# Moving the block-edge part of a short convolution from TensorE to Pool: raw edge tokens as a ninth block, seven taps summed in channel-major form

## The chip, the cores and the metric

One NeuronCore of one Trainium2 chip runs the whole program. The metric is the device time of one execution in microseconds (us), the median of several runs. The profile is taken from one execution; its span (first to last instruction) is some 1.7 us shorter than that execution's time. All runs quoted here are of the state called fast. Engines are named as in the profile: PE (TensorE), PEld (its weight loads), DVE (VectorE), ACT (ScalarE), POOL (GpSimd), SP (the queue that issues most transfers).

## The reference, cut to what matters

```python
# x: 8 x 4096 x 192, weight: 8 heads x 7 taps
w = softmax(weight, axis=-1)
x_pad = 6 zero tokens ahead of each sequence
out[b, s, head] = sum over k of w[head, k] * x_pad[b, s + k, head]   # causal, 7 taps
h = out.reshape(32768, 192) @ w_in       # 192 x 2048
return (h * cos(h)) @ w_out              # 2048 x 192
```

Each output token of the convolution needs the six tokens before it. That is what makes the edge of a block of 128 tokens special: the first six tokens of a block need tokens of the block before.

## The kernel before: the parts that the change touches

A tile is 512 tokens, a unit two tiles (8 blocks of 128 tokens). Per unit the steps are: load `x` and the 16 tokens around each block start; cast to bf16 (Pool); convolve with banded weights (PE); evict to `ct` (ACT copies the result out of PSUM, the memory that PE writes to); double (Pool); transpose by DMA to channel-major `cT`; repair the edges (Pool). Then `mm1` multiplies by `w_in`, ACT and DVE form h cos(h), and the second product runs on PE. Convolution, first product and second product of different tiles are interleaved by hand in `PE_ORDER`.

A convolution matmul sees one block at a time. The six tokens at each block start come out wrong, so the 8 starts of a unit, 16 tokens each, were convolved as a ninth block, and the right values copied over after the transpose:

```python
def mm(i, rows, **flags):
    return conv_mm(u, c, ps, i, sides[rows], 0, UB + 1, ...)        # 9 blocks, 216 columns
...
conv_out(u, c, ps, 0, 0, UB + 1, nc.scalar.copy, banks=(b,))         # ACT evicts 9 blocks

def double_unit(u, n0=0, n1=UB + 1):
    ct = ct_tiles[u]
    nc.gpsimd.tensor_copy(out=ct[:, n0:n1, :, 1, :], in_=ct[:, n0:n1, :, 0, :])

def mend_edges(u):                                                   # "the repair"
    nc.gpsimd.tensor_copy(out=cT[u][:, 0:UB, :, 0 : K - 1],
                          in_=cT[u][:, UB].rearrange("p c (n t) -> p n c t", t=16)[:, :, :, 8 : 8 + K - 1])

PE_ORDER = "h0 m1 c1 m6 c2 m4 h1 m10 h2 p h3 m10 h4 m9 h5 m9 h6 m4 q h7 m11"
```

## Time and profile before

| | before |
|---|---|
| time, median of 3 runs | 715.89 us (715.42 to 716.17) |
| span of the profiled run | 714.0 us |
| PE, DVE, ACT, POOL busy | 99%, 91%, 84%, 21% |
| PE clock granted | full throughout |
| steady tile | 10.83 us |

The prediction below shows the lines on which it rests. Two more views belong beside them. The first lists what PE's matmuls waited for in the whole run (us in total, times, longest us); its largest rows are:

```profile
PE h L349 <- DVE g L360: 1.4, 4, 0.5
PE o_ps L105 <- DVE zero L100: 1.3, 1, 1.3
PE o_ps L190 <- POOL x_bf L179: 0.8, 1, 0.8
```

All of these lie in the first 40 us. The second view is the table of stretches: length and busy time of each engine, then the granted clock (the column before the last two, 1.00 is full), DMA share and GB/s. It covers the moment at which tile 2 begins, in the kernel before:

```profile
34.00:38.00 4.00, 3.52 (x60) 2.56 (x58) 3.72 (x4) 3.80 (x6) 0.50 (x1) 1.00 0.90 113
38.00:43.00 5.00, 5.00 (x80) 3.62 (x78) 4.63 (x5) 4.11 (x5) 0.52 (x2) 1.00 0.89 197
```

### The profile page before, as it was taken

To read this page: it belongs to the slowest core of one execution; us is meant where nothing else is said; L and a number is where in the kernel's file an instruction comes from. 1 tells how busy PE (TensorE), PEld (TensorE's weight loads), DVE (VectorE), ACT (ScalarE), POOL (GpSimd) and SP (SyncE) were. 2 spreads that over 40 slices of the span, in tenths; PEclk is the share of its full clock that TensorE was granted. 3 is DMA by queue.
4 is the path that set the end of the run, shared out by engine and by line. 5 is a ranking of instruction groups with operands and counts; after the bars stand their busy time and mean duration, and the time that the engine had idled before them with its cause. 6 is when DMAs were issued, how large, how long until landed. Compare 5 with 4: busy or idle time off the path is not lost.

```text
span 714.0 us, 26320 instructions
## 1 busy us (share of the span) xinstructions
PE 704.0 (99%) x11826; PEld 539.5 (76%) x11827; DVE 647.6 (91%) x601; ACT 600.7 (84%) x718; POOL 149.4 (21%) x123
## 2 busy tenths in 40 slices
PE   7999999999999999999999999999999999999998
PEld 3577777777777777777777777777777777777776
DVE  7899999999999999999999999999999999999995
ACT  7888888888888888888888888888888888888874
POOL 5622111222102221202221122221022221121000
PEclk9999999999999999999999999999999999999999
DMA  8963554454763444553646543545644545513402
GB/s 215 233 146 85 134 146 107 113 123 97 146 134 103 129 101 119 145 123 100 141 88 133 145 108 111 129 91 145 137 90 138 103 117 146 127 50 90 95 25 68
DMA packets 183696, 85.24 MB, mean 119 GB/s; under 512 B 111648, under 2 KB 183200, under 8 KB 183584
## 3 DMA queue, kind: packets, MB, share of 16 engines
q1 hardware_dynamic: 182872, 82.59, 48.3%
q8 instruction: 92, 1.51, 0.9%
q0 software_dynamic: 416, 0.79, 0.8%
q10 hardware_dynamic: 296, 0.20, 0.1%
q14 instruction: 20, 0.16, 0.1%
HBM read 31.36 MB, written 25.17 MB: 79 GB/s over the span
## 4 chain that ended last, share of the span: by engine, by line
PE 96%; DVE 1%; ACT 1%; DMA 1%; POOL 1%; issue 0%; SPq 0%; POOLq 0%
PE o_ps L393 47%; PE h L349 45%; PE h L190 3%; DMA x_f<-in_x_dram 1%; ACT cs L356 0%; PE h L393 0%; POOL x_bf L179 0%; DVE g L360 0%; DVE band L279 0%; SPq L253 0%; POOL mask L128 0%; ACT mask L133 0%; ACT ct L298 0%; PE o_ps L190 0%; DVE diag L269 0%
## 5 line engine op out<-in xcount | busy, mean ns | idle before, releaser
L360 DVE TENSOR_TENSOR g<-h,cs 128x1024 bf16<-128x1024 f32 (+1 forms) x513 | 608.6, 1218 | 29.1 <-ACT cs L356 25.2
L356 ACT ACTIVATE cs<-h 128x1024 bf16<-128x1024 f32 (+1 forms) x513 | 514.0, 1022 | 99.8 <-PE h L349 93.7
L393 PE MATMUL o_ps<-wo,g 64*128 64x192 bf16 x8128 | 436.6, 243 | 1.2 <-ACT ct L205 0.6
L393 PEld LDWEIGHTS <-g 64*128 64x128 bf16 x8192 | 368.4, 94 | 86.6 <-SPq L164 1.1
L349 PE MATMUL h<-cT,w 64*128 64x512 bf16 (+1 forms) x3078 | 412.4, 376 | 1.9 <-DVE g L360 1.4
L349 PEld LDWEIGHTS <-w 64*128 64x128 bf16 x3078 | 161.1, 94 | 69.2 <-issue 3.4
L259 POOL COPY cT<-cT 128x144 bf16<-128x144 bf16 x31 | 9.5, 307 | 427.6 <-DMA cT<-ct 280.6
L179 POOL CAST x_bf<-x_f 128x1728 bf16<-128x1728 f32 (+1 forms) x32 | 80.4, 2514 | 8.0 <-DMA x_f<-in_x_dram 7.9
L247 POOL COPY ct<-ct 128x1728 bf16<-128x1728 bf16 x31 | 50.4, 1627 | 78.1 <-ACT ct L205 78.1
L404 DVE COPY o_sb<-o_ps 128x384 f32<-128x384 f32 x63 | 35.1, 558 | 26.1 <-PE o_ps L393 25.8
L205 ACT CAST ct<-h 128x432 bf16<-128x432 f32 x120 | 56.5, 522 | 0.6 <-PE h L190 0.3
L190 PE MATMUL h<-x_bf,band 64*128 64x216 bf16 (+1 forms) x472 | 43.4, 253 | 0.0
L404 ACT COPY o_sb<-o_ps 128x384 f32<-128x384 f32 x63 | 29.9, 474 | 1.6 <-PE o_ps L393 1.6
L190 PEld LDWEIGHTS <-band 64*128 64x128 bf16 (+1 forms) x496 | 24.3, 94 | 8.7 <-issue 1.5
L105 PE MATMUL o_ps<-zero 128*128 128x512 bf16 x12 | 4.3, 511 | 1.3 <-DVE zero L100 1.3
L105 PEld LDWEIGHTS <-zero 128*128 128x128 bf16 x15 | 1.5, 115 | 3.0 <-DVE zero L100 1.3
L414 DVE COPY o_sb<-h 128x192 f32<-128x192 f32 x1 | 0.4, 357 | 3.7 <-PE h L393 3.7
L414 ACT COPY o_sb<-h 128x192 f32<-128x192 f32 x1 | 0.3, 318 | 3.8 <-PE h L393 3.8
L461 POOL CAST wo<-wo_f 128x1536 bf16<-128x1536 f32 x2 | 2.9, 1470 | 1.8 <-DMA wo_f<-in_moe_w_out_dram 1.8
L393 PE MATMUL h<-wo,g 64*128 64x192 bf16 x64 | 3.0, 243 | 0.1
L190 PE MATMUL o_ps<-x_bf,band 128*128 128x96 bf16 (+1 forms) x24 | 1.9, 223 | 0.8 <-POOL x_bf L179 0.8
L292 PE MATMUL o_ps<-x_bf,band 128*128 128x48 bf16 x32 | 1.4, 183 | 1.2 <-ACT x_bf L179 0.7
(52 smaller groups left out, 32.3 us busy)
## 6 DMA issues: line engine op xcount, KB each, us to landing
out_dram<-o_sb SPq DMA_DIRECT2D x63, 384.0 KB
x_f<-in_x_dram SPq DMA_DIRECT2D x31, 768.0 KB
x_f<-in_x_dram SPq DMA_DIRECT2D x31, 96.0 KB
wo_f<-in_moe_w_out_dram SPq DMA_DIRECT2D x4, 384.0 KB
x_f<-in_x_dram SPq DMA_DIRECT2D x2, 384.0 KB
w<-in_moe_w_in_dram POOLq DMA_DIRECT2D x2, 384.0 KB, 6.3
cT<-ct SPq DMA_TRANSPOSE x32
out_dram<-o_sb ACTq DMA_DIRECT2D x2, 96.0 KB
```

The source lines that it names most:

```text
L105: nc.tensor.matmul(out=bank, lhsT=zero[:, 0:128], rhs=zero, start=True, stop=True)
L179: copy(out=bf[u][:, n0 + o : n1 + o, :].rearrange("p n (h k r) -> p (n h) k r", k=NC, r=R), in_=x_tiles[u][:, n0:n1, :].rearrange("p n (h ...
L190: return nc.tensor.matmul(out=ps[i // 2][:, 0 : (n1 - n0) * 2 * G].rearrange("p (n k i r) -> p i n k r", n=n1 - n0, k=NC, i=2)[:, i % 2], ...
L205: copy(o[:, :, 0, :], i[:, :, 0, :])
L247: nc.gpsimd.tensor_copy(out=ct[:, n0:n1, :, 1, :], in_=ct[:, n0:n1, :, 0, :])
L259: nc.gpsimd.tensor_copy(out=cT[u][:, 0:UB, :, 0 : K - 1], in_=cT[u][:, UB].rearrange("p c (n t) -> p n c t", t=16)[:, :, :, 8 : 8 + K - 1])
L349: nc.tensor.matmul(out=h[:, i, n0 * 128 : n1 * 128], lhsT=w[rows, k, j, :], rhs=c[rows, m0 + n0 : m0 + n1, k, :], start=(k == 0), stop=(k ...
L356: nc.scalar.activation(out=cs[:, :, part], in_=h[:, :, part], func=AF.Sin, bias=math.pi / 2.0, scale=1.0)
L360: nc.vector.tensor_tensor(out=g_tiles[t][:, 2 * j : 2 * j + 2, part], in0=h[:, :, part], in1=cs[:, :, part], op=ALU.mult)
L393: ms.append(nc.tensor.matmul(out=o_ps[tt, b, si], lhsT=g_tiles[tt][rows, f, s * 128 : (s + 1) * 128], rhs=wo[rows, f // 2, f % 2, :], star ...
L404: copies[b](o_sb[t][:, 2 * b : 2 * b + 2, :].rearrange("p s d -> p (s d)"), o_ps.pop((t, b)))
L461: nc.gpsimd.tensor_copy(out=wo[:, q * HP : (q + 1) * HP], in_=wo_f[:, q * HP : (q + 1) * HP])
```

## The change

The intent: take the ninth block out of PE's matmuls and ACT's evictions, since PE sets the time, and use Pool, which stood idle 79% of the span. The raw edge tokens are copied to `ct` and transposed with the rest; Pool then forms the seven-tap sums of the first six tokens of each block. The taps, by channel, come from two tiny matmuls at the start. The orders of the steady work were adjusted. The core of the diff, with cuts:

```diff
-            return conv_mm(u, c, ps, i, sides[rows], 0, UB + 1, ...)
+            return conv_mm(u, c, ps, i, sides[rows], 0, UB, ...)
-            conv_out(u, c, ps, 0, 0, UB + 1, nc.scalar.copy, banks=(b,))
+            conv_out(u, c, ps, 0, 0, UB, nc.scalar.copy, banks=(b,))
-        nc.gpsimd.tensor_copy(out=ct[:, n0:n1, :, 1, :], in_=ct[:, n0:n1, :, 0, :])
+        nc.gpsimd.tensor_copy(out=ct[:, 0:UB, :, 1, :], in_=ct[:, 0:UB, :, 0, :])
+        for t in range(2):
+            nc.gpsimd.tensor_copy(out=ct[:, UB, :, t, :]..., in_=bf[u][:, UB, :]...)
+    def spread_taps(ps):
+        for i in range(2):
+            nc.tensor.matmul(out=ps, lhsT=pick[:, i]..., rhs=wn[:, i, :], start=i == 0, stop=i == 1, ...)
+        nc.vector.tensor_copy(tap, ps)
     def mend_edges(u):
-        nc.gpsimd.tensor_copy(out=cT[u][:, 0:UB, :, 0 : K - 1], in_=cT[u][:, UB]...[:, :, :, 8 : 8 + K - 1])
+        window = ...                                  # 24 edges x 6 tokens x 7 taps, overlapping
+        nc.gpsimd.tensor_tensor(out=edge_prod, in0=window, in1=tap..., op=ALU.mult)
+        nc.gpsimd.tensor_tensor(out=edge_prod[..., 0:3], in0=edge_prod[..., 0:3], in1=edge_prod[..., 3:6], op=ALU.add)
+        for j in (1, 2):
+            nc.gpsimd.tensor_tensor(out=edge_prod[..., 0], in0=edge_prod[..., 0], in1=edge_prod[..., j], op=ALU.add)
+        nc.gpsimd.tensor_tensor(out=cT[u][:, 0:UB, :, 0 : K - 1]..., in0=edge_prod[..., 0], in1=edge_prod[..., 6], op=ALU.add)
@@ conv_rest (start-up)
+        spread_taps(banks[1][:, 2 * NB * 2 * G :][:, 0:K])
-    PE_ORDER = "h0 m1 c1 m6 c2 m4 h1 m10 h2 p h3 m10 h4 m9 h5 m9 h6 m4 q h7 m11"
-    ACT_ORDER = "s0 ec1 ec2 Q s1 P s2 s3 s4 s5 s6 s7"
+    PE_ORDER = "h0 m4 c1 m6 c2 m4 h1 m7 h2 p h3 m13 h4 m10 h5 m6 h6 m3 q h7 m11"
+    ACT_ORDER = "s0 ec1 Q ec2 s1 P s2 s3 s4 s5 s6 s7"
```

## The prediction

> **What bounds the kernel now.** I read the page first, for shares of the span. Its first and fourth parts:
>
> ```profile
> PE 704.0 (99%) x11826; PEld 539.5 (76%) x11827; DVE 647.6 (91%) x601; ACT 600.7 (84%) x718; POOL 149.4 (21%) x123
> PE 96%; DVE 1%; ACT 1%; DMA 1%; POOL 1%; issue 0%; SPq 0%; POOLq 0%
> ```
>
> TensorE is busy 99% of the span and carries 96% of the chain that ended last. Pool is the idle engine (21%). A busy TensorE isn't proof by itself, since matmul ends are modelled, so next I took the chain in order of time over one steady tile (a tile is 512 tokens, two tiles are one unit of 1024 tokens):
>
> ```profile
> 314.88 0.65 PE h L349 x6
> 315.52 0.08 PE o_ps L393 x2
> 315.61 0.18 PE h L190 x4
> 315.79 0.50 PE o_ps L393 x12
> 316.29 0.18 PE h L190 x4
> 316.47 0.33 PE o_ps L393 x8
> 316.80 0.65 PE h L349 x6
> ```
>
> Here the chain holds nothing but matmuls, back to back: L349 is the first matrix product, L393 the second, L190 the convolution. It also gives true spacings, which the mean durations don't, as two half-array matmuls run side by side. Twelve L393 matmuls of 192 columns take 0.50 us, so a pair takes 83 ns; six L349 of 512 columns take 0.65 us, a pair 217 ns; four L190 of 216 columns take 0.18 us, a pair 92 ns. A tile has 64 pairs of L393, 24 of L349 and 4 of L190: 5.28 + 5.19 + 0.37 = 10.84 us, and the tile before starts at 304.05, 10.83 us earlier. So in the steady part every pair counts and nothing else does. The costs there are spacings of pairs.
>
> Third, the groups by form, for durations on the engines the change touches (busy us and mean ns after the bar):
>
> ```profile
> L205 ACT CAST ct<-h 128x432 bf16<-128x432 f32 x120 | 56.5, 522 | 0.6 <-PE h L190 0.3 <-issue 0.3
> L247 POOL COPY ct<-ct 128x1728 bf16<-128x1728 bf16 x31 | 50.4, 1627 | 78.1 <-ACT ct L205 78.1
> L190 PE MATMUL h<-x_bf,band 64*128 64x216 bf16 x464 | 42.3, 253 | 0.0
> L259 POOL COPY cT<-cT 128x144 bf16<-128x144 bf16 x31 | 9.5, 307 | 427.6 <-DMA cT<-ct 280.6 <-PE h L349 147.0
> ```
>
> Last, Pool in order of time, in the steady part and then near the start, with TensorE beside it at the start. Columns: start us, duration us, what, and idle time before it.
>
> ```profile
> 300.42 0.31 POOL L259 COPY cT<-cT 128x144 bf16<-128x144 bf16 x1 [13.71 <-DMA cT<-ct]
> 300.67 2.57 POOL L179 CAST x_bf<-x_f 128x1728 bf16<-128x1728 f32 x1
> 306.68 1.63 POOL L247 COPY ct<-ct 128x1728 bf16<-128x1728 bf16 x1 [3.12 <-ACT ct L205]
> 322.06 0.31 POOL L259 COPY cT<-cT 128x144 bf16<-128x144 bf16 x1 [13.75 <-DMA cT<-ct]
> ```
>
> ```profile
> 20.52 1.47 POOL L461 CAST wo<-wo_f 128x1536 bf16<-128x1536 f32 x1 [1.78 <-DMA wo_f<-in_moe_w_out_dram]
> 21.93 1.63 POOL L247 COPY ct<-ct 128x1728 bf16<-128x1728 bf16 x1
> 28.20 2.54 POOL L179 CAST x_bf<-x_f 128x1728 bf16<-128x1728 f32 x1 [0.21 <-DMA x_f<-in_x_dram]
> 32.40 0.31 POOL L259 COPY cT<-cT 128x144 bf16<-128x144 bf16 x1 [1.66 <-DMA cT<-ct]
> ```
>
> ```profile
> 32.67 0.82 PE L393 MATMUL o_ps<-wo,g 64*128 64x192 bf16 x16
> 33.33 0.81 PE L349 MATMUL h<-cT,w 64*128 64x512 bf16 x6
> 36.52 0.82 PE L349 MATMUL h<-cT,w 64*128 64x512 bf16 x6 [0.48 <-DVE g L360]
> ```
>
> The steady repair of edges (L259) at 322.06 serves a unit whose first product starts near 336.5 (304.05 + 3 x 10.83): 14 us of slack. The very first repair does not have that. It serves unit 1, waits for that unit's transpose until 32.40, and the first product of tile 2, which reads unit 1, starts at 33.33, only 0.6 us after the repair's end at 32.71. There an instruction on the idle engine is almost on the path.
>
> **What the Trainium skill says.** "TensorE: Matmul & The Clock Gate", section "Back-to-back issue gap", gives an isolated warm gap of N/2.4 + 2.5 ns for N columns: 82.5, 215.8 and 92.5 ns for 192, 512 and 216. The trace's pairs (83, 217, 92) agree. "GPSIMD Engine Reference", section "3.1 Elementwise — side-by-side cycle accounting", gives 4497 ns for a two-input operation of 2048 fp32 elements per partition; no such operation is in this trace. The same page's section 7 adds some 50% per element for reads at a byte step over 8. "SBUF — State Buffer", section "Who interferes with whom", says that VectorE with at most one SBUF input outside the 2-port modes doesn't contend with Pool. VectorE's product L360 reads one operand from PSUM, and the trace agrees: four of them took 4.74 us from 298.35, while Pool cast during the second half, and 4.74 us again from 307.93, most of it with Pool idle.
>
> **The change, part by part.** (1) Convolution matmuls cover 8 blocks and not 9, 192 columns and not 216. A pair gets 10 ns cheaper (24 columns at 2.4 per ns; L393 has this very shape, at 83 ns). 464 half-array matmuls are 232 pairs: 232 x 10 ns = 2.3 us off the path. The 16 full-array ones of the first two tiles lie in a part where TensorE waits anyway: nothing.
>
> (2) ScalarE's evictions shrink from 432 to 384 elements. Its eviction of 384 from PSUM (L404) takes 474 ns against 522: 48 ns x 120 = 5.8 us, on an engine that is 84% busy and off the path: nothing.
>
> (3) The doubling on Pool copies 8 blocks (1536 elements) and adds two copies of 192. From 1728 elements in 1627 ns and 144 in 307 ns: 0.833 ns per element and 187 ns fixed. So 1467 + 2 x 347 = 2161 ns, 0.5 us more than 1.63.
>
> (4) The repair becomes a product of 24 x 6 x 7 = 1008 elements, an addition of 432 and three of 144. An estimate from the GPSIMD page and the fixed 187 ns of this trace: (4497 - 187) / 2048 = 2.10 ns per element. Product 187 + 2117 = 2.30 us; first addition 1.09; the three small ones read every seventh fp32, a step of 28 bytes, so half as much again per element: 187 + 144 x 3.15 = 0.64 each, 1.92 together. Sum 5.3 us; successive Pool instructions overlap by about 0.06 us in this trace, four times: 5.1. Without the stride penalty it is 4.6. I take 4.9 us, against 0.31.
>
> (5) Pool's sum per unit of 21.7 us: 4.9 + 2.55 + 2.16 = 9.6 us against 4.5. That is 44%, and in the steady part the longer repair ends near 327 instead of 322.4, the cast at 329.5, the doubling at 331.7; the transpose that needs it isn't issued before 337.62. No steady wait.
>
> (6) At the start, Pool's work in order: the doubling of unit 1 starts at 21.93 (set by the arrival of wo_f, unchanged) and ends 0.5 us later. The transpose is issued and lands 0.5 us later: 32.9. The repair runs to 37.8. The first product of tile 2 can't start before 37.85 instead of 33.33: 4.5 us. Everything before it on TensorE has room now, so slips there cost nothing more. Is any of it regained? The wait of 0.48 us at 36.52 is for the ring of three h buffers: first product, cosine (ScalarE), multiplication (VectorE), 3.19 us after that product's start. It moves along, so no. After it TensorE has no waits in which to make up time: +4.5 us on the end.
>
> (7) Later start-up: the doubling of unit 2 runs 37.8 to 40.0, its transpose 40.0 to 44.7 (4.72 as now), its repair about 48 to 53; needed at 54.77 + 4.5 = 59.3. The turn of the second product's row halves goes through the same queue as the transpose; it is needed near 47, so it is free. The taps' picking matrix (one memset, two selects, about 1.0 us by the rows of ident and mask) fits Pool's idle 1.66 us before 14.81. The two tiny matmuls and the 0.17 us copy of the taps fall before 33 us, behind the new wait.
>
> (8) The reordering. By the spacings above the ring needs for each product the end of the multiplication three entries earlier; worked through for the new order, the smallest margin is about 0.2 us, as now. It neither gains nor loses.
>
> Sum: -2.3 + 4.5 = +2.2 us: 718.1.
>
> **The rivals.** *The start-up wait isn't there* (a repair as short as 1 us, or a start with slack that I misread): then only the 2.3 us count, 713.6. Against it: 0.6 us between repair and reader, and one final addition that writes all eight blocks that the product reads. For it: the profile shows no two-input Pool operation, so its size is the least certain figure. *Contention*: Pool's longer reads slow VectorE, which is 91% busy; a slowdown by 8% makes VectorE the bound and each per cent beyond costs some 6 us. The equal 4.74 us speak against it. *A cold clock*: TensorE stands for about 4 us before tile 2. "TensorE: Matmul & The Clock Gate", section "What's actually happening", says an idle window of about 3.4 us halves the clock until a busy window has passed; no run shows it here, as the granted clock is full in every slice. A free-running window rarely fits wholly into 4 us; if it does, some 1.7 us more: 720. *Pool slower than the estimate* by 1.5 times: 720.5.
>
> **Range and chances.** The saving is sure to 0.3 us, the wait to about 1.2 us, plus the small chances of no wait and of a cold clock: 715.6 to 719.8. Two per cent is 14.3 us; only strong contention or a serious stall in every unit would reach it, and no gain could.
>
> **What would show it.** Convolution matmuls at 83 ns a pair and a steady tile of 10.79 us show step 1; Pool's product near 2.3 us and a repair near 4.9 us step 4; a single TensorE wait on Pool's repair of some 4 us between 33 and 38 us step 6; multiplications still at 1220 ns the absence of contention. Repeated waits for Pool or a repair under 2 us would prove me wrong.

## The result, and the profile after

The changed kernel takes 719.46 us (median of 6 runs, 719.13 to 719.81) against 715.79 us for the kernel before (6 runs, 715.42 to 716.28). The ratio is 1.0051 with a 95% interval of 1.0038 to 1.0064: slower by half a per cent. Here and below a ratio is the mean time of one kernel's fast runs over that of the other's in the same rounds, so it isn't quite the ratio of the medians.

The page of the changed kernel (span 718.1 us):

```profile
PE 705.2 (98%) x11829; PEld 539.8 (75%) x11829; DVE 646.4 (90%) x602; ACT 590.0 (82%) x718; POOL 305.9 (43%) x312
PE 94%; DMA 2%; POOL 1%; ACT 1%; DVE 1%; issue 1%; SPq 0%; POOLq 0%; ACTq 0%
```

Pool's work has doubled, as meant. In the chain that ended last, PE's share fell from 96% to 94% and the DMA's rose from 1% to 2%; the page doesn't say where. The groups by form show the operations on which the estimate rested (busy us, mean ns):

```profile
L279 POOL TENSOR_TENSOR edge_prod<-cT,tap 128x1008 f32<-128x1008 bf16 x31 | 69.4, 2240 | 349.2 <-DMA cT<-ct 349.2
L190 PE MATMUL h<-x_bf,band 64*128 64x192 bf16 x464 | 40.3, 244 | 0.0
L392 DVE TENSOR_TENSOR g<-h,cs 128x1024 bf16<-128x1024 f32 x511 | 604.6, 1222 | 35.9 <-ACT cs L388 25.3
```

The product takes 2.24 us (2.30 estimated), the convolution matmul now has nearly the duration of the second product's (244 against 243 ns), and VectorE's multiplication is unchanged (1222 against 1220 ns). The place where the time goes is the start of tile 2. First Pool, then PE, in order of time:

```profile
33.11 2.23 POOL L279 TENSOR_TENSOR edge_prod<-cT,tap 128x1008 f32<-128x1008 bf16 x1 [1.70 <-DMA cT<-ct]
35.42 1.01 POOL L282 TENSOR_TENSOR edge_prod<-edge_prod 128x432 f32<-128x432 f32 x1
36.51 1.16 POOL L284 TENSOR_TENSOR edge_prod<-edge_prod 128x144 f32<-128x144 f32 x2
37.74 0.61 POOL L285 TENSOR_TENSOR cT<-edge_prod 128x144 bf16<-128x144 f32 x1
```

```profile
33.98 0.82 PE L425 MATMUL o_ps<-wo,g 64*128 64x192 bf16 x16
38.40 0.82 PE L381 MATMUL h<-cT,w 64*128 64x512 bf16 x6 [3.60 <-POOL cT L285]
39.05 0.36 PE L190 MATMUL h<-x_bf,band 64*128 64x192 bf16 x4
39.21 1.80 PE L425 MATMUL o_ps<-wo,g 64*128 64x192 bf16 x20
```

PE waits 3.60 us for the last addition of the first repair. What follows is the second finding: 20 matmuls of the second product take 1.80 us at 39.21, where in this view 20 of them take 1.00 us in a steady part. The stretches say why. The granted clock (third number from the right) fell:

```profile
18.00:22.00 4.00, 3.22 (x17) 1.36 (x16) 3.65 (x4) 3.23 (x5) 1.90 (x2) 0.60 1.26 158
34.00:38.00 4.00, 0.81 (x18) 0.67 (x15) 1.76 (x2) 1.06 (x2) 3.69 (x5) 1.00 0.29 85
38.00:43.00 5.00, 4.60 (x46) 3.27 (x47) 1.69 (x2) 2.24 (x4) 2.33 (x4) 0.66 0.36 30
```

From 38 to 43 us the mean clock is 0.66, and in the two stretches of a microsecond from 40 to 42 it is 0.50 ("half clock" below). There is also an earlier dip, 0.60 from 18 to 22 us, of which more below. The page's row of 40 slices hides both: with slices of 18 us it prints a 9 throughout.

The steady part, by the chain in order of time (start us, length us):

```profile
310.49 0.17 PE h L190 x4
310.65 0.49 PE o_ps L425 x12
311.15 0.17 PE h L190 x4
...
321.28 0.17 PE h L190 x4
```

Still nothing but matmuls, and from one tile's first convolution piece to the next it is 321.28 - 310.49 = 10.79 us, where it was 315.61 - 304.78 = 10.83 us before. So the intended saving is there, and the loss is a single event in the start-up. The ledger, from the traces:

| us from the span's start | before | after | difference |
|---|---|---|---|
| doubling of unit 1 starts (Pool) | 21.93 | 23.06 | +1.13 |
| first repair starts (transpose landed) | 32.40 | 33.11 | +0.71 |
| first repair ends | 32.71 | 38.35 | +5.64 |
| first product of tile 2 starts | 33.33 | 38.40 | +5.07 |
| fourth product of tile 2 starts | 37.74 | 44.09 | +6.35 |
| end of the span | 714.0 | 718.1 | +4.1 |

Up to the fourth product 6.35 us are lost, 5.07 until tile 2 starts and 1.28 behind that. The 5.07 us aren't all waiting: PE itself came 1.31 us late to the piece ahead of the wait (33.98 and not 32.67), which the wait covers. From there to the end 6.35 - 4.1 = 2.25 us come back. (The two profiled runs differ by 4.1 us, the medians by 3.7; the profiled run of the changed kernel was the slowest of its six.)

### The profile page after: what moved, and what is told of

Read it like the earlier page. It is cut to its first block, busy times and chain, and to the rows that moved or that the text cites. A ratio compares the mean times of both kernels' runs of the same rounds, so it can differ in the third digit from the quotient of the medians.

```text
span 718.1 us, 26526 instructions
## 1 busy us (share of the span) xinstructions
PE 705.2 (98%) x11829; PEld 539.8 (75%) x11829; DVE 646.4 (90%) x602; ACT 590.0 (82%) x718; POOL 305.9 (43%) x312
## 4 chain that ended last, share of the span: by engine, by line
PE 94%; DMA 2%; POOL 1%; ACT 1%; DVE 1%; issue 1%; SPq 0%; POOLq 0%; ACTq 0%
PE o_ps L425 46%; PE h L381 45%; PE h L190 3%; DMA cT<-ct 1%; DMA x_f<-in_x_dram 1%; ACT cs L388 1%; PE h L425 0%; POOL edge_prod L279 0%; DVE g L392 0%; DVE band L306 0%; POOL edge_prod L284 0%; POOL edge_prod L282 0%; POOL mask L128 0%; ACT mask L133 0%; ACT ct L329 0%
## 5 line engine op out<-in xcount | busy, mean ns | idle before, releaser
L392 DVE TENSOR_TENSOR g<-h,cs 128x1024 bf16<-128x1024 f32 (+1 forms) x513 | 605.9, 1220 | 36.9 <-ACT cs L388 26.3
L279 POOL TENSOR_TENSOR edge_prod<-cT,tap 128x1008 f32<-128x1008 bf16 x31 | 69.4, 2240 | 349.2 <-DMA cT<-ct 349.2
L205 ACT CAST ct<-h 128x384 bf16<-128x384 f32 x120 | 51.8, 483 | 8.8 <-PE h L190 5.1
L248 POOL COPY ct<-ct 128x1536 bf16<-128x1536 bf16 x31 | 45.5, 1469 | 0.5 <-ACT ct L205 0.5
L190 PE MATMUL h<-x_bf,band 64*128 64x192 bf16 (+1 forms) x472 | 41.3, 244 | 0.0
L284 POOL TENSOR_TENSOR edge_prod<-edge_prod 128x144 f32<-128x144 f32 x62 | 34.4, 555 | 4.9
L282 POOL TENSOR_TENSOR edge_prod<-edge_prod 128x432 f32<-128x432 f32 x31 | 31.3, 1010 | 2.4
L285 POOL TENSOR_TENSOR cT<-edge_prod 128x144 bf16<-128x144 f32 x31 | 18.9, 609 | 2.4
L250 POOL COPY ct<-x_bf 128x192 bf16<-128x192 bf16 x62 | 19.8, 350 | 0.0
```

Of the source, the lines that this page charges most:

```text
L190: return nc.tensor.matmul(out=ps[i // 2][:, 0 : (n1 - n0) * 2 * G].rearrange("p (n k i r) -> p i n k r", n=n1 - n0, k=NC, i=2)[:, i % 2], ...
L205: copy(o[:, :, 0, :], i[:, :, 0, :])
L248: nc.gpsimd.tensor_copy(out=ct[:, 0:UB, :, 1, :], in_=ct[:, 0:UB, :, 0, :])
L279: nc.gpsimd.tensor_tensor(out=edge_prod, in0=window, in1=tap.rearrange("p (a b k) -> p a b k", a=1, b=1).to_broadcast([128, NC * UB, K - 1 ...
L282: nc.gpsimd.tensor_tensor(out=edge_prod[:, :, :, 0:3], in0=edge_prod[:, :, :, 0:3], in1=edge_prod[:, :, :, 3:6], op=ALU.add)
L284: nc.gpsimd.tensor_tensor(out=edge_prod[:, :, :, 0], in0=edge_prod[:, :, :, 0], in1=edge_prod[:, :, :, j], op=ALU.add)
```

## The experiments

My theory after reading the result had three parts. The first repair holds up tile 2. The half clock after its wait costs 1.3 us more. And the earlier slip of 1.1 us comes from the small copy of the taps. The main rival was that the longer Pool work costs something in every unit. Nine kernels ran, each with five rounds beside the kernel before (five or six runs each). The kernel before had medians of 716.01 us beside the first four, 716.08 beside the next four and 715.87 beside the last.

### 1. Unit 1 in the old way

```diff
-            return conv_mm(..., 0, UB, ...)
+            return conv_mm(..., 0, UB + (u == 1), ...)      # likewise in the full-array matmuls and conv_out
     def double_unit(u):
+        if u == 1: one copy of all nine blocks; return
     def mend_edges(u):
+        if u == 1: the short copy; return
```

> The changed kernel with one unit, unit 1, done as before: nine convolved blocks and the short copy as its repair; all later units as changed. My theory: the whole loss is the first repair, the half clock that follows its wait, and a slip of about 1 us earlier in the start-up, and the steady units gain 2.3 us. Then the first product of tile 2 has no wait on Pool, starts near 34.8 us instead of 38.4, no half-clock stretch follows at 39 to 43 us, and the time is about 715.0 us (713.5 to 715.6), under the kernel before. Rival (the longer Pool work costs in every unit, by contention or late transposes): 717.5 us or more.

Measured: 715.02 us median, ratio 0.9982 (0.9967 to 0.9997). In the profile no PE matmul waits on a repair any more; the short copy starts at 32.78 and takes 0.31 us. But the six runs fall into two groups: three at 713.79 to 713.94 us with a mean clock of 1.000, three at 716.09 to 716.33 with 0.995. The profiled run is one of the latter, with a half clock early on, and tile 2 starts at 36.06 us in it, not near 34.8 as expected:

```profile
22.00:26.00 4.00, 3.67 (x24) 2.35 (x24) 1.70 (x2) 2.73 (x4) 2.24 (x3) 0.50 1.09 301
34.00:38.00 4.00, 4.00 (x72) 3.00 (x70) 2.48 (x3) 3.57 (x6) 2.05 (x3) 1.00 0.53 176
```

What follows: the loss sits in unit 1, as all other units keep the change and half the runs are 2.2 us under the kernel before. The rival of a cost in every unit falls. The early half clock, nearly harmless in the changed kernel because PE waits later anyway, costs 2.4 us once that wait is gone. (That the three faster runs had none is inferred from their mean clock of 1.000; none of them has a trace.) I hadn't expected two groups.

### 2. The copy of the taps on ScalarE

At 14.47 us ScalarE, which was to evict a convolution bank, stood for 1.36 us, and the releaser named is VectorE's copy of the taps:

```profile
15.83 0.86 ACT L203 CAST ct<-o_ps 128x384 bf16<-128x384 f32 x2 [1.36 <-DVE tap L270]
```

The taps lie in unused columns of the same PSUM bank. The Trainium skill, "PSUM — Partial Sum Buffer", section "PSUM bank collisions raise a hardware error", states that two engines may not access one bank, in the same partitions, at the same time, reads against reads included. The program's list of waits agrees: ScalarE's eviction waits for VectorE's semaphore. VectorE's copy, 0.15 us long, stood in line behind its multiplications.

```diff
-        nc.vector.tensor_copy(tap, ps)                       # ahead of the evictions
+        nc.scalar.copy(tap, banks[1]...)                     # behind ScalarE's eviction of that bank
```

> The changed kernel with the copy of the seven taps moved from VectorE, ahead of the evictions, to ScalarE, behind its own eviction of the same bank. My theory: ScalarE's wait of 1.4 us for VectorE near 15 us goes, TensorE's clock doesn't fall to half at 19 to 22 us, the doubling of unit 1 starts near 22.0 us instead of 23.06, the first repair ends about 0.6 us earlier, and the time falls by 0.4 to 0.9 us, to about 718.8. Rival (the early slip came from the transfers of the weights, which landed later, or from the picking matrix on Pool): ScalarE's wait goes, but doubling and repair stay within 0.2 us, and so does the time.

Measured: 719.42 us, ratio 1.0043 (1.003 to 1.0055). The profile came as expected: the doubling starts at 22.08 us, the clock is full from 18 to 22 us, the repair ends at 37.91 instead of 38.35. The time hardly followed: 0.04 us between the medians, 0.26 us when each is compared with the kernel before in its own rounds (3.41 us over it instead of 3.67). In the profile tile 2 starts 0.44 us earlier, but the half clock now covers its first product too (1.21 us instead of 0.82), and by the fourth product (43.74 against 44.09) 0.35 us are left. One run of the five, at 717.52 us, was 1.9 us faster than the others. So this expectation missed in size: the earlier slip was real and nearly worthless as long as a half clock follows. Nor does this profile show that the copy alone made the slip. Experiments 3 and 7 keep the copy and ScalarE's wait of 1.4 us; in their profiled runs the clock stayed full from 18 to 22 us, and the doubling started at 22.22 and 22.05. What goes with the late doubling is the early half clock: the doubling starts at 22.93 to 23.06 us in the four profiled runs that have one (the changed kernel and experiments 1, 4 and 8), at 22.05 to 22.55 in those of the other six experiments.

### 3. Dummy matmuls in the wait

```diff
         h = h_pool.tile([128, 2, T], FP32, name="h")
+        if t == 2 and j == 0:
+            keep_warm(15, h[:, 0, :])        # overwritten by the true product
```

> The changed kernel with 15 dummy matmuls of 512 columns (3.2 us) into the first h buffer of tile 2, in the time in which TensorE waits for the first repair. My theory: the granted clock stays full from 39 to 43 us and the time falls by about 1.3 us (0.8 to 1.8), to 718.2; the wait itself ends at the same moment. Rival (the half clock costs nothing, as the ring of h buffers paces those microseconds): within 0.3 us of the changed kernel.

Measured: 718.0 us, ratio 1.0028 (1.0016 to 1.004), 1.46 us below the changed kernel's median (2.0 us over the kernel before instead of 3.7). The true product starts at 38.23, no earlier to speak of (38.40), and the clock stays full:

```profile
38.23 0.82 PE L383 MATMUL h<-cT,w 64*128 64x512 bf16 x6 [0.93 <-POOL cT L285]
38.87 0.34 PE L190 MATMUL h<-x_bf,band 64*128 64x192 bf16 x4
39.04 1.01 PE L427 MATMUL o_ps<-wo,g 64*128 64x192 bf16 x20
```

The stretch, with a granted clock of 1.00:

```profile
38.00:43.00 5.00, 4.21 (x64) 2.94 (x65) 2.74 (x3) 3.91 (x6) 2.16 (x4) 1.00 0.39 71
```

The fourth product starts at 42.64, 4.41 us after the first, as in the kernel before (37.74 - 33.33 = 4.41); in the changed kernel it was 5.69. So the half clock is 1.28 us of the loss. PE's wait for the ring of h buffers there (0.57 us, 0.48 in the kernel before) doesn't hide it.

### 4. The old orders of the steady work

```diff
-    PE_ORDER = "h0 m4 c1 m6 c2 m4 h1 m7 h2 p h3 m13 h4 m10 h5 m6 h6 m3 q h7 m11"
+    PE_ORDER = "h0 m1 c1 m6 c2 m4 h1 m10 h2 p h3 m10 h4 m9 h5 m9 h6 m4 q h7 m11"     # and ACT_ORDER
```

> The changed kernel with the orders of TensorE's and ScalarE's steady work as before. My theory: the order is worth nothing, within 0.5 us of the changed kernel, a steady tile still 10.79 us. Rival (the order is what lets the longer Pool work or the later convolution fit): at least 2 us slower, with waits of TensorE for VectorE or Pool in every unit.

Measured: 720.07 us, 718.16 to 721.51, ratio 1.0054 (1.004 to 1.0068). The spread of 3.4 us goes only roughly with the mean clock (0.993 to 0.998): the profiled run at 718.16 waited 3.40 us and kept a full clock behind the wait. A difference of 0.6 us can't be read out of this spread, so the comparison was made again in experiment 7.

### 5. Both start-up repairs together

The edits of 1 and 2.

> Both start-up repairs together: unit 1 as before, and the taps copied by ScalarE behind its own eviction; all later units as changed. My theory: no wait on Pool and a full clock from 19 to 27 us in most runs, so that all runs lie where the three faster runs of the first experiment lay: 713.7 (713.3 to 714.2), 2.0 to 2.3 us under the kernel before. Rival (the half clock early in the first experiment was chance and has nothing to do with the taps): two groups of runs again, at 713.8 and 716.2.

Measured: 713.56 us (713.11 to 715.11, five runs, mean clocks 0.999 to 1.000), ratio 0.9969 (0.9957 to 0.9982). It is faster than both kernels, by 2.5 us than the one before. The span is 712.2 us with PE busy 99% of it, and PE in order of time shows that tile 2 starts without a wait, at 33.85:

```profile
33.19 0.82 PE L431 MATMUL o_ps<-wo,g 64*128 64x192 bf16 x16
33.85 0.81 PE L387 MATMUL h<-cT,w 64*128 64x512 bf16 x6
```

None of the five shows the two groups of experiment 1. With five runs against three half-clock runs of six that speaks for the taps' copy as the cause, without proving it: in experiments 3 and 7, with the copy where it was, most runs had no early dip either. All eleven traces allow a count. With the copy on VectorE, four of eight have the early half clock; without it (the kernel before, experiments 2 and 5) none of three. PE is indeed sparser with it: busy for 0.49 to 0.70 us of the two microseconds from 17 to 19 in the eight, for 1.35, 1.28 and 0.84 us in the three. But that alone doesn't decide, as experiment 3's run had the least, 0.49 us, and kept a full clock. That the copy's wait makes a matter of chance likelier fits all of this; it isn't shown.

### 6. The whole repair twice in every later unit

On top of experiment 3, so that the clock doesn't blur the result; repeating the repair changes no value.

```diff
                     mend_edges(u + 1)
+                    mend_edges(u + 1)          # units 2 and later
```

> The kernel with the dummy matmuls of the third experiment, and with the repair done twice in a row for every unit from the second on, which gives the same result. Pool then works some 15 of 21.6 us per unit. My theory: Pool's steady work has slack of more than 5 us, so nothing changes: within 0.4 us of the third experiment's 718.0, and VectorE's multiplication still takes 1220 ns. Rival (Pool's reads cost VectorE or the later transposes cost TensorE): 30 units at 0.2 us or more each, 6 us or more.

Measured: 736.28 us, 18.3 us more than experiment 3. My expectation failed. But the rival's mechanisms aren't seen either: VectorE's multiplication still takes 1222 ns. What PE waits for is the cast on Pool, which its convolution needs, and the queue's transpose waits for Pool's doubling. The waits (us in total, times, longest), PE's and then the queue's:

```profile
PE h L190 <- POOL x_bf L179: 14.8, 13, 1.3
```

```profile
SPq L257 <- POOL ct L250: 41.0, 30, 2.4
```

The chain in order of time shows the shape of it:

```profile
306.48 0.59 POOL ct L250 x2
307.07 0.02 issue
307.08 7.59 DMA cT<-ct
...
324.84 0.61 POOL cT L285
325.45 2.48 POOL x_bf L179
327.93 0.05 issue
327.98 0.25 POOL x_bf L182
328.23 1.40 POOL ct L248
329.63 0.59 POOL ct L250 x2
330.22 0.02 issue
330.24 7.59 DMA cT<-ct
```

Each unit closes a loop: transpose, repair, cast, doubling, next transpose. In the trace Pool takes its work in the program's order, so the repair of one unit stands ahead of the doubling of the next. Here one turn takes 330.24 - 307.08 = 23.16 us, and a unit has 21.57. Not every turn is as long: the starts of the transposes are 21.2 to 23.3 us apart, 22.2 on average from 62.75 to 662.80 us. A turn that begins at 397.31 with a transpose of 6.2 us takes 21.64 us, about what a unit has. In the changed kernel the same loop takes 6.1 us (a transpose landing at 306.15 after its start at 300.02) + 5.2 + 2.55 + 2.1 = 15.9 us, or 17.5 with a transpose of 7.6 us. The slack is 4.0 to 5.6 us, and 5.35 us more used it up. Why a transpose takes 6.1 us in some units and 7.6 in others, I left open.

### 7. The old orders, with the clock held up

The edits of 3 and 4.

> The kernel with the dummy matmuls, with the old orders of TensorE's and ScalarE's steady work. With the clock held up, the orders can be compared without the chance of a half clock. My theory: equal to the third experiment's 718.0 within 0.4 us, a steady tile of 10.79 us in both. Rival (the fourth experiment's median, 0.6 us above the changed kernel, was the order): 718.6 or more.

Measured: 718.22 us, ratio 1.003 (1.0017 to 1.0042), against experiment 3's 718.0 and 1.0028; the two ran on different chips, so the ratios are the better comparison. The reordering is worth nothing that these runs can show.

### 8. A shorter first repair, with a wrong result on purpose

```diff
-        nc.gpsimd.tensor_tensor(... 0:3 += 3:6 ...)
-        for j in (1, 2):
+        if u > 1:
+            nc.gpsimd.tensor_tensor(... 0:3 += 3:6 ...)
+        for j in (1, 2) if u > 1 else ():
```

> Wrong result on purpose: the changed kernel with the three additions between the product and the last addition left out in the first repair alone, which shortens it by 2.3 us (1.01 + 2 x 0.56 us and their gaps). My theory: the end of the first repair sets the start of tile 2, so the wait falls from 3.6 to about 1.3 us, the clock stays full behind it, and the time falls by 2.3 + 1.3 = 3.6 us, to about 715.9 (715.3 to 716.6). Rival (something else, the transpose or the conv of unit 2, holds tile 2 nearly as long): a fall of less than 1.5 us.

Measured: 715.75 us (715.5 to 715.99), the result wrong as intended. The wait shrank to 0.96 us, the clock behind it stayed full:

```profile
35.64 0.82 PE L382 MATMUL h<-cT,w 64*128 64x512 bf16 x6 [0.96 <-POOL cT L286]
```

Taking 2.3 us out of one repair among 31 took 3.7 us off the time. This dose, together with experiment 1, settles that the first repair's end sets the start of tile 2. That the clock behind it is lost or kept with the length of the wait fits the profiled runs: lost after 3.60 and 4.11 us, kept after 3.40 and 0.96.

### 9. Only the product twice in every later unit

```diff
+        for _ in range(2 if u > 1 else 1):
             nc.gpsimd.tensor_tensor(out=edge_prod, in0=window, in1=tap..., op=ALU.mult)
```

> The kernel with the dummy matmuls, and from the second unit on only the repair's product done twice (the same result), 2.3 us more of Pool's time per unit, where the whole repair again was 5.35 us more and cost 18 us. My theory now: Pool's work closes a loop once per unit (transpose to landing 6.1 to 7.7 us, repair 5.2, cast 2.55, doubling 2.1, then the next transpose), 15.9 to 17.6 us of the unit's 21.57, so there are 4.0 to 5.6 us to spare: 2.3 us more change nothing, within 0.4 us of the third experiment's 718.0. Rival (any longer Pool work costs in proportion, by contention): 2.3/5.35 of 18 us, some 7 to 8 us.

Measured: 719.06 us (718.82 to 720.25), ratio 1.0051 (1.0037 to 1.0065) where experiment 3 had 1.0028. It is 1.06 us over experiment 3 by the medians and 1.2 us over it when each is compared with the kernel before in its own rounds (3.19 and 1.99 us over it): outside my 0.4 us, and far from the rival's 7. In the profiled runs (spans 716.7 and 716.6 us) the starts of the transposes run 0.1 us apart throughout, for instance at 277.01 and 276.92, and at 622.30 and 622.21, so nothing accumulates in the steady units; and PE waits on neither cast nor repair there. The 1.06 us of the medians are explained only in part: some 0.4 us of it lie outside the span (time minus span is 2.1 to 2.2 us in all five runs here, 1.6 to 1.8 in experiment 3's), and three of the five runs have a mean clock between 0.995 and 0.998, where experiment 3 had one of five. Why, stays open. The existence of slack is shown, as 2.3 us cost nothing in the steady trace and 5.35 us cost 18; its exact size is an estimate from the loop above.

## Why the prediction was right or wrong

The prediction said 718.1 us (715.6 to 719.8); measured were 719.46 us. Direction, place and most of the mechanism were right. The sum itself was 1.4 us short; that the time still lies inside the range, 0.3 us from its upper end, it owes to the range, which made room for a cold clock that the sum left out. By its own steps:

- Step 1, the saving: predicted 2.3 us. The ledger shows 2.25 us, a steady tile is 10.79 us as foretold, and experiment 5 shows 2.5 us as a whole. Right. One reading was finer than its line: two convolution pairs in 0.18 us are 90 ns a pair, and the 92 ns come close to the formula that they were to confirm. The 10 ns saved per pair came out nonetheless (0.04 us over a tile's four pairs).
- Step 2, ScalarE's shorter evictions worth nothing: they became 39 ns shorter (483 against 522 ns), 48 predicted. The steady chain holds only matmuls, so nothing came of it there. Right.
- Steps 3 and 4, Pool's durations: the doubling and its two copies 1.47 + 2 x 0.35 = 2.17 us (2.16 predicted); product 2.24 us (2.30), first addition 1.01 (1.09), the small ones 0.56, 0.56 and 0.61 (0.64 each). The sum of the five is 4.98 us. The repair took 5.24 us from start to end, 4.9 predicted: I let successive Pool instructions overlap by 0.06 us, but these depend on each other, and there is a gap of about 0.07 us between them.
- Step 5, no steady wait: right for the changed kernel, as no PE matmul waits on Pool after 38.40 us. The reason that I gave, and carried into experiment 6, was too loose: I judged each slack against its own reader and overlooked that the steps form one loop with 4.0 to 5.6 us to spare.
- Step 6, the one delay, by which tile 2 starts later: predicted 4.5 us, measured 5.07 (PE's own wait in it is 3.60). The transpose landed 0.71 us later, not 0.5, and the repair was 0.34 us longer. Step 7 called the tiny matmuls and the copy of the taps harmless; the copy held up ScalarE's eviction of a PSUM bank that both read, by 1.36 us. What that cost is nearly hidden by the wait of tile 2 (experiment 2), and whether it brings on the early half clock isn't shown.
- Step 8, the order neutral: right (experiment 7).
- The cold clock: here the sum is short. The prediction kept it as a rival, with 1.7 us and a small chance ("A free-running window rarely fits wholly into 4 us"). All six runs of the changed kernel have a mean clock of 0.995 to 0.997, where the kernel before mostly has 0.999 to 1.000, and experiment 3 gives back 1.46 us. The mean holds both dips, so it doesn't count the late one by itself; but the late dip is seen in both profiled runs with waits of 3.60 and 4.11 us (the changed kernel and experiment 2) and in neither with 3.40 and 0.96 us (experiments 4 and 8). The step that failed is the guess that a window rarely fits into such a wait: no run of the changed kernel has the mean of 1.000 that a run without a dip shows. It should have stood in the sum: 2.2 + 1.3 = 3.5 us, 719.4. That this meets the measured 719.46 so closely is in part luck, as the delay was 0.57 us larger than predicted and the profiled runs differ by 4.1 us.

## What to carry to other kernels

Work moved to an idle engine is free only where the value has slack. Check the first unit by itself: there the pipeline isn't filled, the slack was 0.6 us where the steady units of the kernel before had 14, and one wait there took more than the saving of all units together. An engine that is 43% busy can still have only a few microseconds to spare per unit, if its in-order queue closes a loop through a transfer. And a wait of PE beyond some 3.5 us (3.60 and 4.11 us lost the clock here, 3.40 us kept it, one profiled run each) should be priced with the half clock that follows; dummy matmuls or, better, the old path for the first unit avoid it.

## What the Trainium skill lacked or had wrong

- "TensorE: Matmul & The Clock Gate", section "What's actually happening", gives an idle window of about 3.4 us as what halves the clock. The waits of 3.60 us (drop) and 3.40 us (no drop) fit it. It gives no figure for how sparse a stretch may be: in the changed kernel PE was busy 0.60, 0.34 and 0.22 us in the three microseconds from 16 to 19 us, with several pauses and none near 3.4 us, and the clock was 0.60 from 18 to 22 us. In experiment 3, with 0.71, 0.18 and 0.31 us busy in the same three, it stayed full, as it did in the kernel before (0.57, 0.58, 0.77).
- "GPSIMD Engine Reference", section "3.1 Elementwise — side-by-side cycle accounting": its figure carries over well to a bf16 input and short overlapping rows (1008 and 432 elements in 2.24 and 1.01 us, so 2.14 ns per element; 2.10 by the prediction's estimate from the page's 4497 ns and this trace's fixed 187 ns). It lacks the gap between dependent Pool instructions, about 0.07 us each, where independent ones overlapped by about 0.06 us. Its section 7 on strided reads fits roughly: 144 elements at a step of 28 bytes took 0.56 us; the line through the two unstrided ones gives 1.01 - 288 x 0.00214 = 0.39 us, so some 0.17 us more.
- "PSUM — Partial Sum Buffer" has the rule that two readers of one bank must not meet. It lacks the price of obeying it: a copy of 0.15 us on a busy engine held up another engine's eviction of the same bank for 1.36 us.
